# A decode step with attention and an MLP: the second MLP matrix at the end of the load stream, nine shared slots, two accumulation groups

## Chip, cores, metric

One core of one Trainium2 chip. The metric is the device time of one execution in microseconds (us), median of several runs. "Span" is the time from the first to the last instruction of the one profiled execution; it is about 1.7 us shorter than the device time. The runs come from several sessions on different chips, each with its own runs of the kernel before (medians 373.60 to 373.92 us), so a ratio compares within a session and medians of different experiments compare across chips to some 0.3 us only. Where a kernel has several runs, the trace is of one of them.

## The reference

Two branches read the same eight rows of width 576 and are mixed by a gate. In short:

```python
q = (x @ wq)                       # 8 rows, 32 heads of 128
k, v = last 2048 positions of the caches, 16 kv heads, each used by 2 heads
a = softmax(q k^T / sqrt(128)) v, all heads side by side, @ wo      # wo: 4096 x 576
b = gelu(layernorm(x) @ w1 + b1) @ w2 + b2                          # w1: 576 x 4608, w2: 4608 x 576
out = g * a + (1 - g) * b,   g = sigmoid(sum(x * gate_w))
```

The K and V windows are 2 x 67 MB; all weights together are about 20 MB. Everything is read once.

## The kernel before

It is written as a list of operations with dependencies that a small planner orders per engine. One queue (SP) issues all large loads, in the order of a list called the stream. K and V arrive in 32 units of 2 MB each, into six slots:

```python
NSLOT = 6
NJ = 4                                    # accumulation in 4 column groups of 144
stream = [("K", i) for i in range(4)] + [("M", i) for i in range(FC)]       # M: chunks of w2
stream += [("K", 4), ("W", 0), ("K", 5), ("W", 1), ("V", 0), ("W", 2), ("K", 6), ("W", 3)]   # W: chunks of wo
# ... then V and K in turn; the last V unit comes in four pieces
slot_free = [[o_qp], [o_qp], [o_qp], None, None, None]   # o_qp: the query projection is done
```

At the start slots 0 to 2 hold `wq` and slots 3 to 5 hold `w1`; `wo` has a region of its own. So the first K unit cannot be issued before the query projection has read `wq`. For each unit of K: VectorE transposes it in two halves, TensorE multiplies it with the query. For each unit of V: 64 matmuls of 8 columns. All that goes into the output (projection, `w2`, bias) is added in one PSUM bank by

```python
for i, (lhsT, rhs) in enumerate(grp.mms):
    for j in range(NJ):
        e.matmul(ps[32 * j:32 * j + 8, BK_ACC, 0:JN], lhsT, rhs[:, JN * j:JN * j + JN], ...)   # JN = 576 / NJ
```

and leaves through one VectorE copy and four output writes, two per queue (the recorded texts call them output loads).

## Time and profile before

373.74 us (373.69 to 373.95). From the page of the profile: the busy time of the engines, the rate of the loads in 40 slices of the span (9.3 us each), and the load queues (packets, megabytes, share of sixteen DMA engines' time).

```profile
PE 254.1 (68%) x3259; PEld 138.9 (37%) x3259; DVE 210.4 (57%) x253; ACT 28.3 (8%) x84; POOL 37.5 (10%) x163
...
GB/s 341 423 395 424 425 423 413 420 419 414 437 430 423 433 433 426 430 430 431 431 426 435 422 431 430 429 431 426 431 433 428 428 433 430 426 428 436 424 413 94
...
q1 hardware_dynamic: 14992, 154.28, 97.9%
q8 instruction: 25, 0.41, 0.4%
```

The rate stands at 413 to 437 GB/s in all but the first, third and last slices, and the packets of the load queue take 97.9% of the sixteen DMA engines' time, so the loads bound the kernel. A 2 MB unit lands every 4.85 us (2.097 MB / 4.85 us = 432 GB/s); this steady rate of the trace is what is called the ceiling below. What can shrink is the start, the end, and single gaps. Note the q8 line: instructions are fetched as 25 blocks of 16 KB.

Two stretches are below the rate. These are windows of the trace: start and end, length, then busy time and instruction count of PE, PEld, DVE, ACT and POOL, then the granted TensorE clock, the mean DMA share and GB/s.

```profile
24.00:30.00 6.00, 3.75 (x65) 3.09 (x62) 0.42 (x1) 1.02 (x1) 2.06 (x11) 1.00 0.89 358
...
360.00:366.00 6.00, 3.21 (x104) 2.74 (x102) 0.00 (x0) 0.00 (x0) 0.00 (x0) 0.50 0.73 302
366.00:372.00 6.00, 1.59 (x40) 1.12 (x40) 0.54 (x2) 0.00 (x0) 0.00 (x0) 0.50 0.07 25
```

The first is a gap: the query projection ends at 24.5 us, the first K loads are issued at 24.71, and before their first 2 MB packets start, at 26.24 us, the data of the load before has run out on most engines (at 26.2 us three load packets are under way, at 25.0 sixteen). The second is the end. Here is the chain of work that ended last (start, length, what):

```profile
344.39 23.61 DMA arena<-in_A_v_cache_dram
368.00 0.05 issue
368.05 0.60 PE ps L673 x16
368.65 0.02 issue
368.68 0.24 DVE arena L695
368.92 0.04 issue
368.96 0.44 PE ps L534 x7
369.40 0.02 issue
369.42 0.31 DVE arena L729
```

The last quarter of the last V unit lands at 368.0 us; then PV, normalisation, projection, eviction and output follow one after the other, to 372.1.

**A second way to read the end.** In these traces a load of 128 rows adds sixteen increments to its semaphore. I read each as one DMA engine whose share has landed; the trace does not name the engine. Their times are in the trace; the last of them is called the landing. The table below is computed from them (first, last, and the difference "spread"; in us from the start of the span):

```
                        first    last   spread
w1, large part          24.77   26.16    1.39
first K unit            31.79   32.67    0.89
last piece of V        362.73  368.00    5.27
```

Between 33 and 368 us the slowest engine has fallen more than 4 us further behind the fastest. The spread does not grow steadily. After a first rise at 38 to 43 us, behind the second and third fetch, it jumps at 146, 166, 176, 264, 284, 294 and 368 us, each time a few us after an instruction fetch (at 143, 161, 173, 261, 280, 292 and 366 us). The fetches in between leave it as it was. The jumps thus follow the first three fetches of every eight. That looked like fetches that take turns over a set of eight engines: a reading of these times, as the trace does not name the engine of a fetch.

### The profile page before, as it was taken

How to read it: one execution, taken by the hardware profiler on the slowest of the kernel's cores; microseconds unless marked ns; L12 is line 12 of the kernel's file. 1: busy time of each engine (PE TensorE's matmuls, PEld its weight loads, DVE VectorE, ACT ScalarE, POOL GpSimd, SP SyncE). 2: the span in 40 equal slices, each digit the busy share in tenths (PEclk: the TensorE clock that was granted, in tenths of full speed). 3: DMA queues.
4: the chain of work that ended last, by engine and by line, in shares of the span. 5: the costliest groups of instructions: out<-in, count | busy, mean ns of one | idle time of the engine just before them, and what ended most of it. 6: DMA issues, size and time to landing. Idle time of an engine off the chain costs nothing.

```text
span 372.1 us, 7310 instructions
## 1 busy us (share of the span) xinstructions
PE 254.1 (68%) x3259; PEld 138.9 (37%) x3259; DVE 210.4 (57%) x253; ACT 28.3 (8%) x84; POOL 37.5 (10%) x163
## 2 busy tenths in 40 slices
PE   0169995661684987496749786877859774987554
PEld 0159432230341553243324443433415332543453
DVE  1414596934159645974468646954585448754600
ACT  1010001100002000200020001100020002000300
POOL 7003011010100110010100110011001010000000
PEclk9999999695865988788886868697659666788855
DMA  8999999999999999999999999999999999999992
GB/s 341 423 395 424 425 423 413 420 419 414 437 430 423 433 433 426 430 430 431 431 426 435 422 431 430 429 431 426 431 433 428 428 433 430 426 428 436 424 413 94
DMA packets 15097, 154.77 MB, mean 416 GB/s; under 512 B 1349, under 2 KB 5462, under 8 KB 6234
## 3 DMA queue, kind: packets, MB, share of 16 engines
q1 hardware_dynamic: 14992, 154.28, 97.9%
q8 instruction: 25, 0.41, 0.4%
q10 hardware_dynamic: 74, 0.03, 0.0%
q14 instruction: 6, 0.05, 0.0%
HBM read 154.30 MB, written 0.01 MB: 415 GB/s over the span
## 4 chain that ended last, share of the span: by engine, by line
DMA 50%; DVE 25%; PE 15%; SPq 8%; issue 1%; DVEq 0%
DMA arena<-in_A_k_cache_dram 37%; DVE arena L629 15%; PE ps L643 11%; DMA arena<-in_B_w_dram 7%; DMA arena<-in_A_v_cache_dram 6%; DVE arena L595 4%; DVE arena L576 4%; SPq L666 3%; SPq L719 2%; PE ps L491 2%; SPq L614 2%; DVE arena L585 1%; DVE arena L579 1%; PE ps L493 1%; PE ps L639 0%
## 5 line engine op out<-in xcount | busy, mean ns | idle before, releaser
L629 DVE STREAM_TRANSPOSE arena<-arena 128x2048 f32<-128x2048 f32 x64 | 145.6, 2298 | 85.8 <-DMA arena<-in_A_k_cache_dram 79.9
L643 PE MATMUL ps<-arena 128*128 128x512 bf16 x512 | 161.8, 476 | 39.0 <-DVE arena L629 39.0
L643 PEld LDWEIGHTS ps<-arena 128*128 128x128 bf16 x512 | 55.5, 115 | 133.5 <-issue 55.0
L673 PEld LDWEIGHTS ps<-arena 128*128 128x128 bf16 x2048 | 56.3, 97 | 13.7 <-DMA arena<-in_A_v_cache_dram 8.5
L673 PE MATMUL ps<-arena 128*128 128x8 bf16 x2048 | 56.7, 166 | 6.8 <-DMA arena<-in_A_v_cache_dram 6.8
L622 POOL COPY arena<-arena 32x32 bf16<-32x32 bf16 x128 | 26.0, 203 | 191.4 <-PE ps L643 175.5
L639 PE MATMUL ps<-arena 128*128 128x512 bf16 x32 | 14.9, 621 | 39.6 <-DVE arena L595 33.1
L576 DVE TENSOR_REDUCE arena<-ps 128x1 f32<-128x2048 f32 x8 | 18.3, 2292 | 27.1 <-PE ps L643 27.1
L590 ACT ACTIVATE arena<-ps,arena 128x512 bf16<-128x512 f32 x32 | 21.5, 685 | 111.2 <-DVE arena L585 111.2
L595 DVE STREAM_TRANSPOSE arena<-arena 128x512 bf16<-128x512 bf16 x32 | 19.9, 676 | 0.9 <-ACT arena L590 0.9
L639 PEld LDWEIGHTS ps<-arena 128*128 128x128 bf16 x32 | 3.5, 127 | 44.7 <-DVE arena L595 33.5
L689 ACT ACTIVATE arena<-ps 128x16 f32<-128x16 f32 x15 | 2.8, 184 | 182.2 <-PE ps L673 182.2
L695 POOL TENSOR_TENSOR arena<-arena 128x16 bf16<-128x16 f32 x15 | 4.0, 264 | 121.3 <-ACT arena L689 106.6
L534 PE MATMUL ps<-arena 128*8 128x144 bf16 (+1 forms) x280 | 8.4, 235 | 6.2 <-POOL arena L695 4.9
L491 PE MATMUL ps<-arena 128*128 128x8 bf16 x144 | 10.9, 201 | 1.7 <-DMA arena<-in_B_w_dram 1.7
L491 PEld LDWEIGHTS ps<-arena 128*128 128x128 bf16 x144 | 10.8, 157 | 2.2 <-DMA arena<-in_B_w_dram 2.2
L413 PE MATMUL ps<-arena 8*128 8x8 bf16 x8 | 0.5, 167 | 12.6 <-DVE arena L386 8.8
L534 PEld LDWEIGHTS ps<-arena 128*8 128x8 bf16 (+1 forms) x280 | 3.9, 84 | 11.3 <-POOL arena L695 5.7
L695 DVE TENSOR_TENSOR arena<-ps,arena 128x16 bf16<-128x16 f32 x1 | 0.2, 228 | 13.6 <-PE ps L673 13.6
L601 DVE RECIPROCAL arena<-ps 128x32 f32<-128x32 f32 x8 | 2.8, 353 | 7.9 <-PE ps L600 7.9
L493 PE MATMUL ps<-arena 128*128 128x8 bf16 x36 | 7.2, 201 | 0.0
L600 PEld LDWEIGHTS ps<-arena 128*128 128x128 f32 x16 | 4.2, 268 | 6.6 <-DVE arena L599 4.5
(78 smaller groups left out, 76.0 us busy)
## 6 DMA issues: line engine op xcount, KB each, us to landing
arena<-in_A_k_cache_dram SPq DMA_DIRECT2D x32, 2048.0 KB, 22.8
arena<-in_A_v_cache_dram SPq DMA_DIRECT2D x31, 2048.0 KB, 24.0
arena<-in_B_w_dram SPq DMA_DIRECT2D x4, 1296.0 KB, 16.1
arena<-in_B_w_dram SPq DMA_DIRECT2D x1, 4608.0 KB, 24.4
arena<-in_A_wo_dram SPq DMA_DIRECT2D x4, 1152.0 KB, 17.6
arena<-in_A_wq_dram SPq DMA_DIRECT2D x1, 4096.0 KB, 12.8
arena<-in_A_v_cache_dram SPq DMA_DIRECT2D x4, 512.0 KB, 21.9
arena<-in_B_w_dram SPq DMA_DIRECT2D x1, 576.0 KB, 25.6
```

Of the source, the lines that this page charges most:

```text
L491: ins = e.matmul(out_, lhsT, yT[:, kt, :], start=(kt == 0), stop=False)
L493: ins = e.matmul(out_, lhsT, yT[:, 4 + c // 2, :], start=False, stop=True)
L534: ins = e.matmul(ps[32 * j:32 * j + 8, BK_ACC, 0:JN], lhsT, rhs[:, JN * j:JN * j + JN], start=False, stop=True, skip_group_check=True, til ...
L576: mx = add("dve", lambda e: e.tensor_reduce(out=k(MX), in_=ps[:, 0:4, :].rearrange("p a n -> p (a n)"), axis=AXL.X, op=ALU.max), deps=[qk_ ...
L590: return e.activation(out=Pm[:, 512 * c:512 * c + 512], in_=ps[:, c, :], func=ACTF.Exp, bias=k(NB), scale=SCALE, accum_out=k(SUM + c))
L595: pts.append(add("dve", (lambda c=c: lambda e: e.transpose(PT[:, g % 2, 16 * c:16 * c + 16, :].rearrange("p r m -> p (r m)"), Pm[:, 512 * ...
L622: return e.tensor_copy(dst, src)
L629: tr = add("dve", (lambda h=h, kb=kb: lambda e: e.transpose(bass.AP(arena_f, offset=foffs("KT") + kb * 2048, ap=[[AST // 2, 128], [1, 2048]]),
L639: mm = e.matmul(ps[:, rc, :], maskL, maskR, start=True, stop=False)
L643: mm = e.matmul(ps[:, rc, :], qbd[:, ub, 2 * h + ee, :], rhs, start=False, stop=(q == 3 and h == 1 and ee == 1))
L666: d = dma("sp", (lambda pp=pp, w=w: lambda e: e.dma_start(slot(s)[:, pp * w:(pp + 1) * w], src[:, :, pp * w:(pp + 1) * w]))(), ("t%d" % pp ...
L673: mm = e.matmul(ps[:, BK_OS[item % 2], 8 * (q % 2):8 * (q % 2) + 8], slot(s)[:, r * 128:(r + 1) * 128], PT[:, g % 2, r, 8 * q:8 * q + 8], ...
```

## The change

`w2` (5.3 MB) moves from near the start to the very end of the stream, with the bias before it. `wo` loses its own region: its four chunks pass through the slots, each behind the V units that it belongs to. The freed memory makes nine slots, and three of them are free from the start. The output is accumulated in two column groups of 288 instead of four of 144, and evicted by two engines at once. The bias matmul, which stood ahead of the query projection, now waits for a bias load behind the last projection chunk. The small piece of `wq` is loaded before the large one. The intent: fewer instructions, a shorter tail, and a stream that never waits.

```diff
-    NSLOT = 6
+    NSLOT = 9
-    NJ = 4
+    NJ = 2
-        stream = [("K", i) for i in range(4)] + [("M", i) for i in range(FC)]
-        stream += [("K", 4), ("W", 0), ("K", 5), ("W", 1), ("V", 0), ("W", 2), ("K", 6), ("W", 3)]
+        stream = [("K", i) for i in range(5)]
...                     (K and V in turn, a chunk of wo after every eighth V unit)
+        stream += [("B", 0)] + [("M", i) for i in range(FC)]
-        slot_free = [[o_qp], [o_qp], [o_qp], None, None, None]
+        slot_free = [[o_qp]] * 3 + [[o_hp]] * 3 + [[]] * 3
-            return (0, 1, 2, 0)[n] if n < 4 else (n - 3) % NSLOT
+            return (n + 6) % NSLOT
-        d_wqm = ...                                  # 4 MB, first
-        d_wqr = ... after=[d_wqm]
+        d_wqr = ...                                  # 0.5 MB, first
+        d_wqm = ... after=[d_wqr]
+            cuts = [0, 4, 7, 9] if ci == FC - 1 else [0, FJ]      # the last w2 chunk in three pieces
-        o_fin = add("dve", ... tensor_copy(out_sb[0:104, :], ps[0:104, BK_ACC, 0:JN]) ...)    # then 4 output writes
+        for j, (eng, ev) in enumerate((("sp", "dve"), ("act", "act"))):                       # one each
...                     (cut: an output tile per head pair, bias rows on 8 partitions, gate load in two)
```

More of the change, by code (lines that the diff above doesn't have):

```diff
@@ L183, in build_kernel @@
     NG = Hkv // HG
-    NSLOT = 6
+    NSLOT = 9
     SE = 4 * W
-    LEAD = 7
     FC, FJ = 4, 9
@@ L189, in build_kernel @@
     FCW = 128 * FJ
-    W2P = 5376
     WOP = 768
-    NJ = 4
+    NJ = 2
+    WO_CH = 8
     JN = D // NJ
@@ L245, in build_kernel @@
         req("o32", 2 * 16, F32)
-        req("oT", 2 * 16, BF)
+        req("oT", Hkv * 16, BF)
         req("out_sb", JN, BF)
@@ L250, in build_kernel @@
         req("KT", 2 * SE // 2, BF)
-        req("wo", Hq * WOP, BF, 512)
         req("RAW", NSLOT * SE, BF, 512)
@@ L294, in build_kernel @@
         b1T = view("b1T")
-        b2_sb = view("b2", 1)
+        b2_sb = view("b2", 8)
         u_sb, uh_sb, v1_sb, v2_sb = view("u"), view("uh"), view("v1"), view("v2")
         hT = view("hT").rearrange("p (t b) -> p t b", b=8)
-        ob = view("ob", 1)
-        ot32 = view("ot32", 1)
+        ob = view("ob", 8)
+        ot32 = view("ot32", 8)
         gb = view("gb")
@@ L305, in build_kernel @@
         o32 = view("o32").rearrange("p (u m) -> p u m", u=2)
-        oT = view("oT").rearrange("p (u h b) -> p u h b", u=2, h=2)
+        oT = view("oT").rearrange("p (u h b) -> p u h b", u=Hkv, h=2)
         out_sb = view("out_sb")
@@ L309, in build_kernel @@
         Pm = view("P")
-        wo_sb = view("wo").rearrange("p (t c) -> p t c", t=Hq)
         RAW = view("RAW")
@@ L325, in build_kernel @@
         w1_r = RAW[:, W1O + 4 * F:W1O + 4 * F + F // 2]
-        w2_sb = RAW[:, 3 * SE:3 * SE + FC * W2P].rearrange("p (c k) -> p c k", c=FC)
         def col(i, parts=128):
@@ L340, in build_kernel @@
         eng_sems = {e: es.enter_context(nc.semaphore("sem_" + e)) for e in ENGS}
-        dma_keys = ["x", "b", "wq", "w1", "wo", "out", "outb"] + ["w2_%d" % i for i in range(FC)] + ["s%d" % i for i in range(NSLOT)] + ["t%d" % i for i in range(4)]
+        dma_keys = ["x", "b", "b2", "wq", "w1", "out", "outb"] + ["s%d" % i for i in range(NSLOT)] + ["t%d" % i for i in range(4)]
         dma_sems = {k: es.enter_context(nc.semaphore("dma_" + k)) for k in dma_keys}
@@ L370, in build_kernel @@
         d_x = dma("act", lambda e: e.dma_start(x_sb, x2), "x", 8 * D * 2, name="d_x")
-        d_gw = dma("act", lambda e: e.dma_start(gw_sb, gate_w.partition_broadcast(8)), "x", 8 * D * 2, name="d_gw", after=[d_x])
+        d_gw, d_gw1 = [dma("act", (lambda r0=r0, r1=r1: lambda e: e.dma_start(gw_sb[r0:r1, :], gate_w.partition_broadcast(r1 - r0)))(), "x", (r1 - r0) * D * 2, name="d_gw%d" % r0, after=[d_x])
+                       for r0, r1 in ((0, 6), (6, 8))]
         d_b1 = dma("act", lambda e: e.dma_start(b1c, B_b1.rearrange("(c f) -> c f", c=FC)), "b", F * 2, name="d_b1", after=[d_gw])
-        d_b2 = dma("act", lambda e: e.dma_start(b2_sb, B_b2.rearrange("(o d) -> o d", o=1)), "b", D * 2, name="d_b2", after=[d_b1])
-        dx = [d_x, d_gw]
-        db = [d_b1, d_b2]
-        d_wqm = dma("sp", lambda e: e.dma_start(wq_m.rearrange("p t c -> p (t c)"), A_wq[0:512, :].rearrange("(p t) c -> p (t c)", t=4)), "wq", 512 * 8192, name="d_wqm")
-        d_wqr = dma("sp", lambda e: e.dma_start(wq_r, A_wq[512:576, :].rearrange("k (s c) -> (k s) c", s=2)), "wq", 64 * 8192, name="d_wqr", after=[d_wqm])
+        dx = [d_x, d_gw, d_gw1]
+        db = [d_b1]
+        d_wqr = dma("sp", lambda e: e.dma_start(wq_r, A_wq[512:576, :].rearrange("k (s c) -> (k s) c", s=2)), "wq", 64 * 8192, name="d_wqr")
+        d_wqm = dma("sp", lambda e: e.dma_start(wq_m.rearrange("p t c -> p (t c)"), A_wq[0:512, :].rearrange("(p t) c -> p (t c)", t=4)), "wq", 512 * 8192, name="d_wqm", after=[d_wqr])
         dwq = [d_wqm, d_wqr]
-        d_w1m = dma("sp", lambda e: e.dma_start(w1_m.rearrange("p t c -> p (t c)"), B_w1[0:512, :].rearrange("(p t) c -> p (t c)", t=4)), "w1", 512 * F * 2, name="d_w1m", after=[d_wqr])
+        d_w1m = dma("sp", lambda e: e.dma_start(w1_m.rearrange("p t c -> p (t c)"), B_w1[0:512, :].rearrange("(p t) c -> p (t c)", t=4)), "w1", 512 * F * 2, name="d_w1m", after=[d_wqm])
         d_w1r = dma("sp", lambda e: e.dma_start(w1_r, B_w1[512:576, :].rearrange("k (s c) -> (k s) c", s=2)), "w1", 64 * F * 2, name="d_w1r", after=[d_w1m])
@@ L441, in build_kernel @@
         o_gb = add("dve", lambda e: e.tensor_copy(gb, ps[:, BK_X, 384:400]), deps=[o_gp], name="gb_ev", cost=0.15)
-        o_obh = add("dve", lambda e: e.tensor_copy(ob[:, 0:8], gb[0:1, 8:16]), deps=[o_gb], name="ob_hi", cost=0.12)
+        o_obh = add("dve", lambda e: e.tensor_copy(ob[:, 0:8], dg[:, 8:16]), deps=[o_dgb], name="ob_hi", cost=0.12)
         o_ob32 = add("dve", lambda e: e.tensor_copy(ot32, ob[:, 0:8]), deps=[o_obh], name="ob_32", cost=0.12)
-        o_obl = add("dve", lambda e: e.tensor_tensor(out=ob[:, 8:16], in0=gb[0:1, 8:16], in1=ot32, op=ALU.subtract), deps=[o_ob32], name="ob_lo", cost=0.12)
+        o_obl = add("dve", lambda e: e.tensor_tensor(out=ob[:, 8:16], in0=dg[:, 8:16], in1=ot32, op=ALU.subtract), deps=[o_ob32], name="ob_lo", cost=0.12)
         o_i32 = []
@@ L541, in build_kernel @@
         NUQ = 4 * NG
-        stream = [("K", i) for i in range(4)] + [("M", i) for i in range(FC)]
-        stream += [("K", 4), ("W", 0), ("K", 5), ("W", 1), ("V", 0), ("W", 2), ("K", 6), ("W", 3)]
-        ki, vi = 7, 1
+        stream = [("K", i) for i in range(5)]
+        ki, vi = 5, 0
         while ki < NUQ or vi < NUQ:
-            if vi < NUQ:
-                stream.append(("V", vi)); vi += 1
             if ki < NUQ:
-                stream.append(("K", ki)); ki += 1
-        WO_CH = 8
-        d_woc = []
+                stream.append(("K", ki))
+                ki += 1
+            if ki >= 6:
+                stream.append(("V", vi))
+                if (vi + 1) % (NUQ // (Hq // WO_CH)) == 0:
+                    stream.append(("W", vi // (NUQ // (Hq // WO_CH))))
+                vi += 1
+        stream += [("B", 0)] + [("M", i) for i in range(FC)]
         last_dma = [d_w1r]
-        slot_free = [[o_qp], [o_qp], [o_qp], None, None, None]
+        slot_free = [[o_qp]] * 3 + [[o_hp]] * 3 + [[]] * 3
         n_slot = [0]
@@ L658, in v_unit, with pv_fn @@
             item = 2 * g + q // 2
-            final = (i == NUQ - 1)
-            src = src_of(A_v_cache, g, q)
-            parts = 4 if final else 1
-            prev = None
-            for pp in range(parts):
-                nr = 64 // parts
-                w = nr * 128
-                d = dma("sp", (lambda pp=pp, w=w: lambda e: e.dma_start(slot(s)[:, pp * w:(pp + 1) * w], src[:, :, pp * w:(pp + 1) * w]))(),
-                        ("t%d" % pp) if final else ("s%d" % s), 4 * W * Dh * 2 // parts, deps=slot_free[s] if pp == 0 else [], name="dv%d_%d" % (i, pp), after=last_dma[-1:])
-                last_dma.append(d)
-                def pv_fn(e, pp=pp, nr=nr):
-                    mm = None
-                    for r in range(pp * nr, (pp + 1) * nr):
-                        mm = e.matmul(ps[:, BK_OS[item % 2], 8 * (q % 2):8 * (q % 2) + 8], slot(s)[:, r * 128:(r + 1) * 128], PT[:, g % 2, r, 8 * q:8 * q + 8],
-                                      start=(q % 2 == 0 and r == 0), stop=(r == 63), skip_group_check=True)
-                    return mm
-                deps = [d] + pt_done[g]
-                if q % 2 == 0:
-                    deps += [o_item_ev[item - 2]] if item >= 2 else [o_qT, o_u]
-                prev = add("pe", pv_fn, deps=deps, name="pv%d_%d" % (i, pp), cost=2.2 / parts, after=[prev] + pv_hist[-1:])
+            d = dma("sp", lambda e: e.dma_start(slot(s), src_of(A_v_cache, g, q)), "s%d" % s, 4 * W * Dh * 2, deps=slot_free[s], name="dv%d" % i, after=last_dma[-1:])
+            last_dma.append(d)
+            def pv_fn(e):
+                mm = None
+                for r in range(64):
+                    mm = e.matmul(ps[:, BK_OS[item % 2], 8 * (q % 2):8 * (q % 2) + 8], slot(s)[:, r * 128:(r + 1) * 128], PT[:, g % 2, r, 8 * q:8 * q + 8],
+                                  start=(q % 2 == 0 and r == 0), stop=(r == 63), skip_group_check=True)
+                return mm
+            deps = [d] + pt_done[g]
+            if q % 2 == 0:
+                deps += [o_item_ev[item - 2]] if item >= 2 else [o_qT, o_u]
+            prev = add("pe", pv_fn, deps=deps, name="pv%d" % i, cost=2.2, after=pv_hist[-1:])
             pv_hist.append(prev)
@@ L686, in v_unit @@
                 hl = q // 2
-                pj = [proj_ops[item - 2]] if item >= 2 else []
                 if item < Hkv - 1:
@@ L690, in v_unit @@
                     o_item_ev[item] = ev
-                    eng, src_, deps = "pool", o32[:, item % 2, :], [ev, rg_done[g]] + pj
+                    eng, src_, deps = "pool", o32[:, item % 2, :], [ev, rg_done[g]]
                 else:
-                    eng, src_, deps = "dve", ps[:, bk, 0:16], [prev, rg_done[g]] + pj
+                    eng, src_, deps = "dve", ps[:, bk, 0:16], [prev, rg_done[g]]
                 def om_fn(e):
-                    return e.tensor_tensor(out=oT[:, item % 2, :, :].rearrange("p h b -> p b h"), in0=src_.rearrange("p (b h) -> p b h", h=2),
+                    return e.tensor_tensor(out=oT[:, item, :, :].rearrange("p h b -> p b h"), in0=src_.rearrange("p (b h) -> p b h", h=2),
@@ L696, in om_fn @@
                                            in1=rg[:, g % 2, 16 * hl:16 * hl + 16].rearrange("p (b h) -> p b h", h=2), op=ALU.mult)
                 oT_done[item] = add(eng, om_fn, deps=deps, name="oT%d" % item, cost=0.25, prio=9)
-                mms = [(oT[:, item % 2, h, :], wo_sb[:, 2 * item + h, 0:D]) for h in range(2)]
-                proj_ops[item] = AccGroup("proj%d" % item, mms, [oT_done[item]] + d_woc, cost=0.6, after=[g_.op for g_ in acc_groups[-1:]], prio=2).op
-        o_m2 = [AccGroup("m2_b", [(ob[:, 0:8], b2_sb), (ob[:, 8:16], b2_sb)], db + [o_obl, o_obh], cost=0.6).op]
@@ L703, in m2_chunk, with wo_chunk @@
-        def m2_chunk(ci):
-            d = dma("sp", lambda e: e.dma_start(w2_sb[:, ci, 0:FJ * D], B_w2[FCW * ci:FCW * ci + FCW, :].rearrange("(p j) n -> p (j n)", j=FJ)),
-                    "w2_%d" % ci, FCW * D * 2, deps=[o_hp], name="d_w2_%d" % ci, after=last_dma[-1:])
-            last_dma.append(d)
-            mms = [(hT[:, FJ * ci + j, :], w2_sb[:, ci, j * D:(j + 1) * D]) for j in range(FJ)]
-            o = AccGroup("m2_%d" % ci, mms, [o_hT, d], cost=2.5, after=o_m2[-1:]).op
-            o_m2.append(o)
-            for s in range(3, 6):
-                slot_free[s] = [o]
+        def wo_chunk(i):
+            s = take_slot()
+            h0 = WO_CH * i
+            dst = slot(s)[:, 0:WO_CH * WOP].rearrange("p (t c) -> p t c", t=WO_CH)
+            d = dma("sp", lambda e: e.dma_start(dst[:, :, 0:D], A_wo[128 * h0:128 * (h0 + WO_CH), :].rearrange("(t p) c -> p t c", p=128)),
+                    "s%d" % s, WO_CH * 128 * D * 2, deps=slot_free[s], name="d_wo%d" % i, after=last_dma[-1:])
+            last_dma.append(d)
+            ops = []
+            for item in range(h0 // 2, (h0 + WO_CH) // 2):
+                mms = [(oT[:, item, h, :], dst[:, 2 * item + h - h0, 0:D]) for h in range(2)]
+                ops.append(AccGroup("proj%d" % item, mms, [oT_done[item], d], cost=0.5).op)
+            slot_free[s] = ops
@@ new lines, in build_kernel, with bias @@
+        o_m2 = []
+        def bias(i):
+            d = dma("sp", lambda e: e.dma_start(b2_sb, B_b2.partition_broadcast(8)), "b2", 65536, name="d_b2", after=last_dma[-1:])
+            last_dma.append(d)
+            o_m2.append(AccGroup("m2_b", [(ob[:, 0:8], b2_sb), (ob[:, 8:16], b2_sb)], [d, o_obl, o_obh], cost=0.6).op)
+        def m2_chunk(ci):
+            s = take_slot()
+            dst = slot(s)[:, 0:FJ * D]
+            src = B_w2[FCW * ci:FCW * ci + FCW, :].rearrange("(p j) n -> p (j n)", j=FJ)
+            cuts = [0, 4, 7, 9] if ci == FC - 1 else [0, FJ]
+            ops = []
+            for n, (j0, j1) in enumerate(zip(cuts, cuts[1:])):
+                d = dma("sp", (lambda j0=j0, j1=j1: lambda e: e.dma_start(dst[:, j0 * D:j1 * D], src[:, j0 * D:j1 * D]))(),
+                        ("t%d" % n) if ci == FC - 1 else ("s%d" % s), 128 * (j1 - j0) * D * 2, deps=slot_free[s] if n == 0 else [], name="d_w2_%d_%d" % (ci, n), after=last_dma[-1:])
+                last_dma.append(d)
+                mms = [(hT[:, FJ * ci + j, :], dst[:, j * D:(j + 1) * D]) for j in range(j0, j1)]
+                ops.append(AccGroup("m2_%d_%d" % (ci, n), mms, [o_hT, d], cost=0.25 * (j1 - j0), after=o_m2[-1:]).op)
+                o_m2.append(ops[-1])
+            slot_free[s] = ops
@@ L713, in build_kernel @@
         pv_hist = []
         for kind, i in stream:
-            if kind == "M":
-                m2_chunk(i)
-            elif kind == "W":
-                h0 = WO_CH * i
-                d = dma("sp", (lambda h0=h0: lambda e: e.dma_start(wo_sb[:, h0:h0 + WO_CH, 0:D], A_wo[128 * h0:128 * (h0 + WO_CH), :].rearrange("(t p) c -> p t c", p=128)))(),
-                        "wo", WO_CH * 128 * D * 2, name="d_wo%d" % i, after=last_dma[-1:])
-                last_dma.append(d)
-                d_woc.append(d)
-            elif kind == "K":
-                k_unit(i)
-            else:
-                v_unit(i)
+            {"K": k_unit, "V": v_unit, "W": wo_chunk, "M": m2_chunk, "B": bias}[kind](i)
@@ L728, in build_kernel, with ev_fn @@
         acc_ops = [g_.op for g_ in acc_groups]
-        o_fin = add("dve", lambda e: e.tensor_copy(out_sb[0:104, :], ps[0:104, BK_ACC, 0:JN]), deps=acc_ops, name="fin", cost=0.3, prio=9)
         fin = []
-        for j in range(NJ):
-            eng = "sp" if j % 2 == 0 else "act"
-            fin.append(dma(eng, (lambda j=j: lambda e: e.dma_start(out2[:, JN * j:JN * j + JN], out_sb[32 * j:32 * j + 8, :]))(), "out" if j % 2 == 0 else "outb", 8 * JN * 2, deps=[o_fin], name="d_out%d" % j, after=last_dma[-1:]))
+        for j, (eng, ev) in enumerate((("sp", "dve"), ("act", "act"))):
+            def ev_fn(e, j=j, ev=ev):
+                dst, src = out_sb[32 * j:32 * j + 8, :], ps[32 * j:32 * j + 8, BK_ACC, 0:JN]
+                if ev == "dve":
+                    return e.tensor_copy(dst, src)
+                return e.activation(out=dst, in_=src, func=ACTF.Copy)
+            o_fin = add(ev, ev_fn, deps=acc_ops, name="fin%d" % j, cost=0.4, prio=9)
+            fin.append(dma(eng, (lambda j=j: lambda e: e.dma_start(out2[:, JN * j:JN * j + JN], out_sb[32 * j:32 * j + 8, :]))(), "out" if j == 0 else "outb", 8 * JN * 2, deps=[o_fin], name="d_out%d" % j, after=last_dma[-1:]))
```

## The prediction

> **What bounds the kernel now.** The load stream. The page's slices move 413 to 437 GB/s from the fourth to the last but one; DVE (57% busy) and PE (68%) have slack. [...] (a 2 MB K or V unit lands every 4.85 us, 432 GB/s). 154.77 MB at that rate are 358 us of the 372.1 us span. The change moves the same bytes, so only the other 14 us can shrink.
>
> **Where the 14 us are** (landing increments and packet records of the trace):
> - Head: first weight packet at 2.36 us; the first 32 KB round takes 2.0 us against 1.21 later.
> - A gap at 25 to 27 us (358 GB/s in the 24 to 30 us window): the first K loads issue at 24.7 us, after the query projection, because every slot lies under a weight matrix. Most engines lose about 0.7 us.
> - Skew between the 16 DMA engines: a unit's increments spread over 0.9 us at the start, 5.3 us at the end, in steps after 16 KB instruction fetches (25, which seem to rotate over eight engines). The last V quarter lands at 368.0 us while half the engines are idle from 363 us.
> - Tail from there: 0.60 PV, 0.23 DVE, 0.41 projection, 0.31 eviction, two output issues per queue (0.75 us), end at 372.1: 4.1 us.
>
> **What the change does.**
> 1. Slots 6 to 8 are free from the start, so three K loads queue behind the first MLP matrix: the 25 us gap goes. Worth 0 to 0.7 us; the slowest engine hardly saw it.
> 2. Small wq piece first (4 KB rows): the first round may be quicker, 0 to 0.3 us.
> 3. Accumulation in two column groups of 288 instead of four of 144: 140 matmuls and as many weight loads fewer, one 16 KB fetch fewer. The fetch at 366.6 us should go, with the last step of the skew: 0 to 0.8 us.
> 4. Tail: after the last landing, four matmuls of 288 columns (estimate 0.55 us, from 0.41 us for eight of 144), two parallel evictions (0.4), one output issue per queue (saves 0.35). The last PV, normalisation and projection move off the tail, behind 5.3 MB of second-matrix loads. 4.1 becomes about 3.0 us: saves 1.1 us.
> 5. Nine slots instead of six: nothing in the steady state, which is at its ceiling. Projection chunks (393 GB/s by landing) cost 3.0 us each wherever they stand. The bias load and matmul are hidden.
>
> All of 1 to 4 lie on the critical path but overlap in part: about 2.3 us.
>
> **Prediction: 371.4 us, 8 in 10 between 370.0 and 372.9. Faster by over 2%: 0.03; within 2%: 0.95; slower by over 2%: 0.02.**
>
> **What would show each step right or wrong.** (1) The 24 to 30 us window should show about 430 GB/s. (3) 24 instruction fetches, final spread about 4.5 us. (4) From the last second-matrix landing to the end about 3.0 us. (5) K and V units still land 4.85 us apart; PE and DVE busy nearly unchanged, DMA mean 417 to 419 GB/s.
>
> **What would make it wrong.** A slot held by a projection chunk until late projections run could stall the queue (a dip below 400 GB/s near 100, 180, 260 or 340 us). The PE order could put a projection before its chunk has landed, and stop QK behind it. The second matrix's matmuls at the halved clock could lag the stream at the end. Fetches could fall on the slowest engine once more, giving back 0.7 us or more. A gain over 2% would need the per-unit 4.85 us to fall, which I see no reason for.

The sum: 0 to 0.7, 0 to 0.3, 0 to 0.8 and 1.1 us, put at about 2.3 us together. The ranges are my estimates. The 0.4 us for the two evictions stands there without a source; they then took 0.40 and 0.45 us in the changed kernel.

## The result

371.22 us (371.06 to 371.26) against 373.72: faster by 0.7%, ratio 0.9931 with a 95% interval of 0.9914 to 0.9948. That is clear of the noise, and within 2%. A ratio here is the mean time of one kernel's runs over that of the other's in the same rounds, so it is not quite the ratio of the medians quoted. In a later session the same kernel took 371.46 us against 373.69.

The page of the changed kernel, the lines that answer to those before:

```profile
PE 242.0 (65%) x3089; PEld 137.5 (37%) x3117; DVE 210.0 (57%) x253; ACT 28.6 (8%) x85; POOL 37.5 (10%) x163
...
GB/s 343 426 422 424 427 432 431 434 424 431 429 431 429 413 436 427 429 427 429 435 426 429 414 431 432 431 431 426 426 435 433 418 424 427 435 429 426 413 420 167
...
q1 hardware_dynamic: 14848, 154.29, 98.5%
q8 instruction: 24, 0.39, 0.4%
```

One instruction fetch fewer, the third slice at 422 instead of 395, the rest as it was. (A few TensorE records are missing here.) The windows:

```profile
24.00:30.00 6.00, 2.40 (x41) 2.43 (x41) 0.00 (x0) 0.08 (x1) 3.25 (x16) 1.00 0.97 404
...
360.00:366.00 6.00, 5.17 (x44) 2.59 (x46) 0.00 (x0) 0.00 (x0) 0.00 (x0) 0.50 0.65 268
366.00:372.00 6.00, 1.11 (x14) 0.52 (x10) 0.45 (x1) 0.40 (x1) 0.00 (x0) 0.82 0.01 2
```

And the end of the chain of work that ended last:

```profile
348.28 14.82 DMA arena<-in_B_w_dram
363.11 0.04 issue
363.15 3.98 PE ps L530 x36
367.13 0.03 issue
367.15 0.05 DVEq L153
367.20 0.04 issue
367.25 0.45 DVE arena L734
```

The tail reads differently now. Before, it hung on the last landing. Now the last landing is at 366.30 us, but the chain leaves the loads at 363.1 and stays on TensorE: 36 matmuls back to back, the third and fourth chunk of `w2`, most of them at half clock (0.50 in the window). TensorE has become the last to finish.

From the landing increments, the 2.61 us of span (372.12 to 369.51) add up as follows (the tail is the time from the last landing to the end):

```
                                   before    after   gain
w1 lands, fastest engine            24.77    24.48   0.29   head
first K unit, fastest engine        31.79    30.77   1.02   head 0.29 + gap 0.73
last load, fastest engine          362.73   361.69   1.04   nothing more in 331 us
last load, slowest engine          368.00   366.30   1.70   + spread 5.27 -> 4.60, 0.67
from there to the end                4.12     3.21   0.91   tail
```

So: 0.3 us head, 0.7 us gap, 0.7 us spread, 0.9 us tail. This is bookkeeping of two traces, and the split between the fastest engine and the spread is loose: the repetition below has 362.12 and 4.27 in place of 361.69 and 4.60. The slowest engine repeats better and gives the same sum another way. Against the repetition it is 0.1 us late at the first K unit of the kernel before, 0.8 us at the third (43.29 against 42.47) and 1.6 us at the end, after the last jump of 0.8 us. The experiments ask whether the causes are the ones named.

### The profile page after: what moved, and what is told of

Read it like the earlier page. It is cut to its first block, busy times and chain, and to the rows that moved or that the text cites. A ratio compares the mean times of both kernels' runs of the same rounds, so it can differ in the third digit from the quotient of the medians.

```text
span 369.5 us, 7044 instructions
## 1 busy us (share of the span) xinstructions
PE 242.0 (65%) x3089; PEld 137.5 (37%) x3117; DVE 210.0 (57%) x253; ACT 28.6 (8%) x85; POOL 37.5 (10%) x163
## 3 DMA queue, kind: packets, MB, share of 16 engines
q1 hardware_dynamic: 14848, 154.29, 98.5%
## 4 chain that ended last, share of the span: by engine, by line
DMA 63%; PE 20%; DVE 13%; SPq 2%; issue 1%; DVEq 0%
DMA arena<-in_A_k_cache_dram 42%; PE ps L641 12%; DMA arena<-in_B_w_dram 11%; DMA arena<-in_A_v_cache_dram 10%; DVE arena L627 9%; PE ps L663 3%; DVE arena L574 2%; PE ps L487 2%; SPq L716 1%; PE ps L530 1%; PE ps L637 1%; SPq L657 1%; PE ps L489 1%; DVE arena L577 0%; DVE arena L593 0%
## 5 line engine op out<-in xcount | busy, mean ns | idle before, releaser
L641 PE MATMUL ps<-arena 128*128 128x512 bf16 x491 | 144.6, 449 | 45.1 <-DVE arena L627 44.0
L641 PEld LDWEIGHTS ps<-arena 128*128 128x128 bf16 x512 | 52.5, 109 | 129.2 <-DVE arena L627 53.2
L663 PEld LDWEIGHTS ps<-arena 128*128 128x128 bf16 x2048 | 56.1, 97 | 19.1 <-DMA arena<-in_A_v_cache_dram 14.2
L637 PE MATMUL ps<-arena 128*128 128x512 bf16 x25 | 12.3, 630 | 40.2 <-DVE arena L593 36.7
L637 PEld LDWEIGHTS ps<-arena 128*128 128x128 bf16 x32 | 3.5, 128 | 42.9 <-DVE arena L593 38.5
L530 PE MATMUL ps<-arena 128*8 128x288 bf16 (+1 forms) x140 | 14.7, 377 | 3.1 <-DMA arena<-in_B_w_dram 1.9
L487 PEld LDWEIGHTS ps<-arena 128*128 128x128 bf16 x144 | 10.8, 160 | 5.0 <-DMA arena<-in_B_w_dram 5.0
L530 PEld LDWEIGHTS ps<-arena 128*8 128x8 bf16 (+1 forms) x140 | 7.1, 106 | 10.9 <-DMA arena<-in_B_w_dram 3.6
(79 smaller groups left out, 79.4 us busy)
```

The costliest lines, as they stand in the source:

```text
L487: ins = e.matmul(out_, lhsT, yT[:, kt, :], start=(kt == 0), stop=False)
L530: ins = e.matmul(ps[32 * j:32 * j + 8, BK_ACC, 0:JN], lhsT, rhs[:, JN * j:JN * j + JN], start=False, stop=True, skip_group_check=True, til ...
L637: mm = e.matmul(ps[:, rc, :], maskL, maskR, start=True, stop=False)
L641: mm = e.matmul(ps[:, rc, :], qbd[:, ub, 2 * h + ee, :], rhs, start=False, stop=(q == 3 and h == 1 and ee == 1))
L663: mm = e.matmul(ps[:, BK_OS[item % 2], 8 * (q % 2):8 * (q % 2) + 8], slot(s)[:, r * 128:(r + 1) * 128], PT[:, g % 2, r, 8 * q:8 * q + 8], ...
```

## The experiments

All are edits of the changed kernel and give correct results. Since single effects are a few tenths of a per cent, I compare landings in the profiled run first and times second. In each table the yardstick is the unaltered changed kernel.

### The yardstick

> The changed kernel unaltered, as the yardstick for the other runs on this chip. Expected 371.2 us against 373.7 of before, a ratio of 0.993; 24 instruction fetches, the last load landing spread over 4.6 us between the DMA engines.

371.46 us (371.09 to 371.86, five runs), ratio 0.9946. First K unit at 30.81 us on the fastest engine, last load at 366.38 us, spread 4.27, tail 2.99 us. Repetition thus moves the last landing by 0.1 us on the slowest engine and 0.4 on the fastest, the spread by 0.3 and the time by up to 0.4 from the median. The trace of the yardstick is of its fastest run, 371.09 us.

### What closed the gap at 25 us?

In the changed kernel the query projection ends at 21.3 us, 3.2 us earlier than before: the small loads of the second queue land earlier (the load of `b1`, for which TensorE waited until 13.5 us, now lets it go at 11.6, 1.9 us), and the bias matmul no longer stands ahead of it in TensorE's order (the other 1.3 us). Loads issued on its end would then come in time even without free slots. Two edits tell these apart.

```diff
 e1:  slot_free = [[o_qp]] * 3 + [[o_hp]] * 3 + [[o_qp]] * 3      # was [[]] * 3 at the end
 e8:  as e1, and four idle VectorE operations (0.75 us each) that the query projection waits for
```

> The changed kernel, but slots 6 to 8 count as free only when the query projection is done, as all slots did before. Theory A, of the prediction (the free slots close the gap at 25 us): the gap comes back, the first K unit lands 0.7 us later on the fastest engine, and the kernel takes 371.7 to 371.9 us. Theory B (the gap closed because the query projection now ends at 21.3 us instead of 24.5, so that K loads issued on its end come in time anyway): no gap, 371.2 us within 0.1.

> As e1, and four idle vector operations of about 0.75 us delay the query projection by 3 us, to where it ended before. Both theories expect the gap back here: the first K unit 0.7 us later, 371.8 to 372.0 us, if most engines pass their loss on to the end. If only the slowest engine matters and it had no gap, 371.2 to 371.4 us. With e1 at 371.2 and e8 at 371.9, theory B stands and the free slots are only a second cure of the same gap.

```
                  median   ratio     first K, fastest   last load, slowest   tail
yardstick         371.46   0.9946         30.81               366.38         2.99
e1                372.17   0.9957         30.98               366.67         3.78
e8                373.67   1.0001         32.59               368.46         3.39
before            373.69                  31.79               368.00         4.12
```

e8, the window of the gap:

```profile
24.00:30.00 6.00, 5.48 (x114) 5.00 (x112) 0.42 (x1) 1.02 (x1) 1.42 (x7) 1.00 0.81 314
```

Without free slots the gap stays closed but for 0.2 us (theory B; the first K load is issued at 22.63 us there); it opens when the projection is late as well. The padding run below (e6, 128 matmuls) has the projection late (its end lets go the next K loads at 28.10 us) and the free slots kept, and its first K unit lands at 30.83: no gap. So either cure is enough, and the change contains both. e1's median is 0.7 us up, and the intervals of the two ratios overlap (0.9946 to 0.9969, and 0.9933 to 0.9959). Its profiled run is 1.1 us above the yardstick's: 0.3 in the landing and 0.8 in the tail, which is treated below.

e8 also settles a point of the prediction. Its gap is wider than that of before (first loads issued at 25.57 us instead of 24.71), and the slowest engine loses 1.75 us at the first K unit and still 2.1 us at the last load. In this run, then, the gap in the stream was not made good later. That the slowest engine "hardly saw it" does not hold in the trace of the kernel before either, past the first unit: against the yardstick it is late, head included, by 0.11 us at the first K unit, but by 0.61 at the second and 0.82 at the third.

### The instruction fetches

```diff
 e3:  NJ = 4, with the eviction and the four output writes of before (about 280 TensorE instructions more)
 e6:  a block of 128 (or 32) useless matmuls into an unused bank, ahead of the query projection
```

> The changed kernel, but accumulating in four column groups of 144 with one eviction and four output loads as before, which brings back some 280 instructions of TensorE. Theory of the prediction: 25 fetches instead of 24, the last spread 0.7 us wider (5.3 instead of 4.6), and the tail after the last landing 0.2 to 0.4 us longer (second output issue): 372.1 to 372.3 us. Rival (the number of fetches does not matter, only the tail does): 371.4 to 371.6 us with the spread at 4.6.

> The changed kernel with 128 useless matmuls (256 TensorE instructions, about 4 us) ahead of the query projection, in time where TensorE waits and the stream has K loads queued in the free slots. Fetch theory: one instruction fetch more (25), falling near 355 to 360 us on the same engine as the first, ninth and seventeenth; the last spread grows by about 1.0 to 1.3 us, and the kernel takes 372.3 to 372.8 us where the unaltered one took 371.4. Rival (what the fewer matmuls gave was TensorE time or a shorter tail): no difference, 371.3 to 371.6 us. If the free slots do close the gap, the first K unit lands at 30.8 us although the query projection is late.

> Control for the padding: 32 useless matmuls (64 instructions) in the same place, too few for one fetch more before the stream ends. Fetch theory: 24 fetches, spread 4.3 to 4.6 us, 371.3 to 371.6 us. If each added instruction costs in itself, a quarter of what the 128 cost.

The queue line of the page, of the three in this order:

```profile
q8 instruction: 26, 0.43, 0.4%
```

```profile
q8 instruction: 25, 0.41, 0.4%
```

```profile
q8 instruction: 25, 0.41, 0.4%
```

```
              median  ratio   fetches ended before  spread   last load,   last load,   tail
                              the last load landed           fastest      slowest
yardstick     371.46  0.9946         24              4.27      362.12       366.38     2.99
e3            372.87  0.9979         25              5.78      361.97       367.75     3.20
pad of 128    373.14  0.9984         25              5.25      362.47       367.72     3.65
pad of 32     371.84  0.9945         24              4.33      362.02       366.35     3.78
```

This is the clearest result. One fetch more while the stream is still running, whether by real work (e3, at 360 us) or by padding alone, puts the slowest engine's last landing back by 1.37 and 1.34 us, while the fastest engine's moves by -0.15 and +0.35. In the control the twenty-fifth fetch starts at 365.84 us, half a microsecond before the last landing: no effect on landings. The first two edits share only that they add some 260 to 280 TensorE instructions, in different places and for different work. That it is the fetch, and not the instructions as such, is seen in time. In e3 the spread goes from 4.36 to 5.80 us with the fetch at 360 us. In the padding run the slowest engine is 0.1 us ahead of the yardstick's at the landing at 346 us, 0.5 behind after the fetch at 345 and 1.3 behind after the one at 355. So the fetches are shown to be a cause of the spread. The spread jumps by 1.2 to 1.5 us at the ninth and seventeenth fetch (1.18 and 1.19 in the first trace of the changed kernel, 1.33 and 1.36 in the yardstick, 1.45 and 1.49 in e3); I read that as the least that a fetch of 16 KB costs the DMA engine that carries it. A 16 KB packet of data takes 0.61 us and the packet of the fetch itself 0.88 to 0.97 (the traces of the kernel before and of the changed one). As an estimate from these jumps, eight engines with three such fetches each, of 24, come to some 4 us, which is the lag at the end: in the yardstick's last load eight increments come at 362.12 to 363.98 us and eight at 366.11 to 366.38. From the loads of this kernel, whose packets take 98.5% of the DMA engines' time, the fetch is not hidden.

The fetches are not all of one price for the end: as I read it, what counts is whether the engine that pays is last, or becomes last by it. In the kernel before the spread jumped with three of every eight, in e3 by over 0.3 us with one of every eight only.

### Head, stream order, number of slots

```diff
 e2:  the 4 MB piece of wq first, as before
 e5:  w2 and the bias behind the fifth K unit; the last wo chunk before the last V unit; last V unit in four pieces
 e4:  NSLOT = 6
```

> The changed kernel, but the 4 MB piece of the query weights goes first, as before. Theory of the prediction: the first round of 32 KB packets takes 2 us again, the first MLP matrix lands 0.2 to 0.3 us later, and so does everything after: 371.6 to 371.8 us where the unaltered one took 371.4. Rival: nothing, the head is hidden.

> The changed kernel with nine slots, two column groups and interleaved projection chunks, but the second MLP matrix is loaded early (behind the fifth K unit) and V ends the stream, its last unit in four pieces as before. Theory: the last load lands at the same time within 0.3 us, and the tail holds PV, normalisation and projection again, 0.5 to 0.9 us more than 3.1: 372.0 to 372.4 us. Rival (the order of the stream changes the stream itself): the last landing moves by over 0.5 us.

> The changed kernel with six slots instead of nine, all of them under a weight matrix at the start. Theory of the prediction (depth gives nothing in the steady state): units still land 4.85 us apart, no stall; as e1 then, 371.4 to 372.2 us. Rival (the nine slots keep the queue full where six would not, since projection chunks now hold slots as well): gaps of over 0.3 us between landings, over 372.5 us.

```
              median  ratio   last load, fastest   last load, slowest   tail
yardstick     371.46  0.9946       362.12               366.38          2.99
e2            371.62  0.9946       362.25               366.74          3.04
e5            372.19  0.9958       361.94               366.40          4.06
e4            372.59  0.9973       363.87               368.52          3.10
```

**e2.** The weights land 0.24 us later, as expected; at the end that is 0.1 to 0.4 us, and in the times it drowns in the scatter (ratios equal). The head is real in the landings and not proven in the times.

**e5.** The order of the stream as such does not move the last landing (366.40 against 366.38). It moves the tail, by 1.1 us. Its last instructions:

```profile
366.45 0.59 PE L673 MATMUL ps<-arena 128*128 128x8 bf16 x16 [0.61 <-DMA arena<-in_A_v_cache_dram]
367.07 0.23 DVE L695 TENSOR_TENSOR arena<-ps,arena 128x16 bf16<-128x16 f32 x1 [15.80 <-PE ps L673]
...
367.36 0.65 PE L530 MATMUL ps<-arena 128*8 128x288 bf16 x4 [0.32 <-DVE arena L695]
368.04 0.45 DVE L752 CAST arena<-ps 8x288 bf16<-8x288 f32 x1 [0.74 <-PE ps L530]
```

PV, normalisation and projection again stand between landing and eviction. Moving the second matrix behind them is worth about a microsecond against the yardstick's tail of 2.99 us, but only 0.3 us against the tails of 3.78 us that other runs show (see the clock below). The prediction's 1.1 us was for this and the two evictions and output writes together; e5 has those already, so the agreement is in size only.

**e4.** Six slots cost 1.1 us in the median (across chips) and 2.1 us at the last landing of the profiled run, which was the slowest of its five (373.35 us); the prediction did not foresee it. It is not the steady state: units land 4.85 us apart in both. On the slowest engine the yardstick and e4 part at one place, the unit whose first share lands at 84 us in the yardstick: its last lands at 86.16 us there and at 88.27 in e4, and from there on e4 is 2.1 us late, to the end. The window there, of e4 and then of the yardstick:

```profile
78.00:84.00 6.00, 5.91 (x85) 3.46 (x85) 5.23 (x3) 0.18 (x1) 1.07 (x5) 1.00 0.98 369
```

```profile
78.00:84.00 6.00, 6.00 (x118) 3.92 (x115) 5.23 (x3) 0.19 (x1) 1.42 (x7) 1.00 1.00 426
```

And the issues of e4's queue ahead of it:

```profile
57.40 0.54 SPq L612 DMA_DIRECT2D arena<-in_A_k_cache_dram  x1
65.92 0.54 SPq L657 DMA_DIRECT2D arena<-in_A_v_cache_dram  x1
76.93 0.54 SPq L612 DMA_DIRECT2D arena<-in_A_k_cache_dram  x1
```

Two issues 11 us apart, where a unit takes 4.85 us to load: the slot waits for VectorE, which is held up by the first softmax, and with six slots the queue then holds no more than the rest of one unit, which lands at 79.77 to 81.49 us. Five of the first 16 KB packets of the late unit, at 79.4 to 79.6 us, take 1.4 to 2.7 us each. No other 16 KB packet between 30 and 340 us takes over 1.2 us in this trace. Why the late unit starts so slowly is not shown. The nine-slot kernel has such waits too (issues at 65.1 and 75.6 us), with three more units queued in front of them. The kernel before may not have needed this, since its 10 MB of `w2` and `wo` in the early stream gave the compute time to catch up; the nine slots would then be the price of moving those loads away. No run with six slots and the early loads kept tests that.

### The tail and the clock of TensorE

Over the runs that end with `w2`, leaving out the fillers below and e3 (other instructions), the tail after the last landing is either 3.0 to 3.2 us or 3.65 to 3.8 us (and 3.4 once), with almost the same instructions. The last matmuls in the timeline of the yardstick, and of e1:

```profile
363.23 3.72 PE L530 MATMUL ps<-arena 128*8 128x288 bf16 x36 [0.75 <-DMA arena<-in_B_w_dram]
```

```profile
363.56 4.49 PE L530 MATMUL ps<-arena 128*8 128x288 bf16 x36 [0.77 <-DMA arena<-in_B_w_dram]
```

And a window inside them, again of the yardstick and of e1 (the clock is the last figure but two):

```profile
366.00:367.00 1.00, 0.95 (x16) 0.44 (x10) 0.00 (x0) 0.00 (x0) 0.00 (x0) 0.99 0.00 0
```

```profile
366.00:367.00 1.00, 1.00 (x12) 0.57 (x10) 0.00 (x0) 0.00 (x0) 0.00 (x0) 0.50 0.05 18
```

The same 36 matmuls take 3.72 us where the clock is granted in full from 366 us, and 4.49 us where it stays at half. The clock records of the traces hold two values, 0.50 and 1.00, and all changes of the clock within one trace lie whole multiples of 3.41 us apart, on a grid that falls differently in each (the first change on record is at 44.06 us in the kernel before and at 42.16 in the changed kernel). In the yardstick a step of this grid falls at 366.02 us, 2.8 us into the matmuls, and the clock rises. In e1 the steps fall at 365.59 us, 2.0 us into them, without a rise, and at 369.00 us, after their end. What makes the clock rise is not shown. It goes with work, without a sharp limit: in the traces of the kernel before and of the changed one all 38 rises follow a step of the grid in which TensorE (matmuls or weight loads) was busy for a share of 0.71 or more, and of the 39 steps after which the clock stayed at 0.50, 38 have a share of 0.69 or less and one has 0.80. In these runs, the later the rise comes after the last landing, the longer the tail was: 2.99 us for a rise 0.36 us before it, 3.21 for 0.12 after, 3.39 for 0.43, 3.65 for 0.98, 3.78 for 1.36 (yardstick, changed kernel, e8, pads of 128 and 32).

### Two attempts at a faster version

If the end is set by engines that lag, and always the same ones, bytes can be moved to the others; so I reasoned. First, which are they? In the trace a load of few rows, n, adds one increment at the issue and n as the data lands (the bias load of the changed kernel, of 8 rows: one at 317.64 us and eight from 349.38 to 353.65). I took it that n engines carry it, and that a load of one row more uses the same engines and one more. This is an assumption: the trace does not name the engines.

```diff
 e7:   loads of 2, 3, ... 15 rows of 128 bytes, each with its own semaphore, before the bias load
 e9:   w1[.., 8192:18432] in rows 0-111, then 112-116, 117-121, 122-126 (five rows each), then row 127
 e10:  as e9, and 4 filler matmuls of 512 columns ahead of the first three chunks of w2 (1, 1, 2)
```

> The changed kernel with fourteen tiny loads of 2 to 15 rows just before the bias load near the end, each with a semaphore of its own, so that their increments show how far behind each DMA engine is[...]. Fetch theory: about eight engines lag by 3 to 4.6 us and the others by under 1.5 us, and the laggards are a fixed set; if they are mostly the higher-numbered ones, shifting bytes to the lower ones would bring the end forward. Rival: the lag is spread evenly over all, with no set to be named. No change of time expected beyond 0.5 us.

> The changed kernel, but 16 of the 128 rows of a 20 KB wide part of the first MLP matrix are loaded five at a time[...]. Theory (the time is set by the DMA engines that lag, and the lag is a fixed set): the last load lands 0.5 to 0.8 us earlier, at 365.6 to 365.9 us, the final spread falls to 3.5 to 3.9, and the kernel takes 370.6 to 370.9 us where the unaltered one took 371.4. Rival (the engines share one limit, so moving bytes moves nothing): 371.3 to 371.6 us.

> As e9, and four filler matmuls of 512 columns fill TensorE's waits between the chunks of the second MLP matrix, so that its clock is granted in full before the last chunk. In the runs so far the tail after the last landing was 3.0 to 3.2 us where the clock came up before the end and 3.7 to 3.8 us where it did not. Theory: tail 2.6 to 2.9 us in every run, the runs scatter less, 370.0 to 370.5 us. Rival (the tail is set by the evictions and output writes alone): as e9.

Five increments of a small load came early, and if loads of five rows always go to those five engines, the other eleven have 20 KB each less to carry. That is some 0.77 us, an estimate from the 0.61 us of a 16 KB packet. In e10, that filling TensorE's waits brings its clock up is likewise a theory.

**e7 (one look).** By what each load adds to the one before, about 350 us, with the engines numbered from 0 in the order in which the loads add them: engines 0 to 4, 7 and 8 were at 349.4 to 351.6 us, 10 at 352.3, and 5, 6, 9 and 11 to 14 at 353.6 to 353.8. Seven are clearly late and an eighth is half-way, which fits fetches that take turns over eight engines, with the third turn of the eighth, the 24th fetch at 352.3 us, still to come. 15 was not probed, but is early by elimination: the chunk of `wo` just ahead has eight increments at 349.2 to 351.4 us, one at 352.2 and seven at 353.4 to 353.6. The numbering stands on the assumption of nested loads. The probe also carries a warning: in it each tiny load delayed its engines by about 0.18 us, though it moved 128 bytes per row. Fourteen of them brought the final spread down to 1.98 us, and yet the last landing was 0.9 us later (367.30): the nested loads held back the early engines most, which narrowed the spread, but the late engines 5 and 6 too, nine or ten times each.

**e9** failed: 379.81 us, ratio 1.0159. The windows of the head:

```profile
18.00:24.00 6.00, 5.06 (x156) 4.37 (x152) 0.43 (x1) 0.38 (x1) 0.00 (x0) 1.00 1.02 290
24.00:30.00 6.00, 0.00 (x0) 0.00 (x0) 0.00 (x0) 0.64 (x1) 3.27 (x16) 1.00 1.13 195
30.00:36.00 6.00, 0.00 (x0) 0.00 (x0) 0.00 (x0) 0.00 (x0) 0.00 (x0) 1.00 0.91 137
```

The engines are busy all through (share 1.02, 1.13, 0.91) at 137 to 290 GB/s. Already while the load of 112 rows is under way the rate falls (205 to 328 GB/s between 19 and 26 us), and further under the five-row loads after it (108 to 153 GB/s between 28 and 36 us); the first K unit is 9 us late. In the first two of those windows the changed kernel, with the 128-row form, ran at 396 and 404 GB/s. Why the rate falls is not shown, nor which of the two shapes costs how much. The final spread was 4.10. Whether moving bytes can help is therefore untested: the edit broke something larger than it mended.

**e10** carries the same fault (377.89 us), so its time says nothing. Its fillers did in the profiled run what they were for:

```profile
367.00:368.00 1.00, 0.85 (x13) 0.54 (x14) 0.00 (x0) 0.00 (x0) 0.00 (x0) 0.73 0.92 389
368.00:369.00 1.00, 1.00 (x12) 0.34 (x8) 0.00 (x0) 0.00 (x0) 0.00 (x0) 1.00 1.01 421
```

The clock came up in it almost six microseconds before the last landing (367.55 and 373.42 us), TensorE then waited for the pieces again, and the tail was 2.87 us against 3.75 in e9. One trace each; the fillers alone, in the kernel that wins, were not run and stay an open proposal. An estimate of their worth from these two tails is up to 0.9 us, on those executions whose clock stays down. No version tried beats the changed kernel.

## Why the prediction was right

Forecast 371.4 us (370.0 to 372.9) and "within 2%" at 0.95; measured 371.22. The sum was 2.3 us; the medians differ by 2.5, the spans by 2.6. That it came so close is in part luck: gap, head and fetches came out at or near the top of their ranges, the tail less than forecast, and a clock that stays down would have added some 0.6 us (3.78 against 3.21). Two times in it stand 0.5 to 0.6 us later than in the trace (the first weight packet starts at 1.82 us, the last fetch at 366.01); nothing rests on them. The terms:

1. **Gap, "0 to 0.7 us".** It gained 0.7, at the top of the range. The reason for the low end of the range was wrong ("the slowest engine hardly saw it"): by the third K unit the slowest engine had lost 0.8 us, head included, and e8 shows that such a loss lasts. And the free slots are only one of two cures; the earlier query projection is the other (e1), which the prediction did not see, and in the change itself the two cannot be told apart. Its check, 430 GB/s in the 24 to 30 us window, failed (404), although the landings show no gap: 4.85 us from the last part of `w1` (25.92) to the first K unit (30.77) on the fastest engine. Landings were the better test.
2. **Head, "0 to 0.3".** 0.29 in the traces, 0.24 at the same landing in e2; not resolved in the times. The first sixteen 32 KB packets take 1.21 to 1.41 us each in the changed kernel, 1.43 to 2.18 before.
3. **Fetches, "0 to 0.8".** 24 fetches and a spread of 4.60, as forecast (4.5); 0.67 us (1.0 against the repetition). Confirmed twice by adding one back, which cost more (1.3 to 1.4) than its removal had gained. That is no contradiction: in the kernel before, the last fetch fell on an engine that was not the last one, so that part of its cost did not show. In the increments of the piece before, one of the eight late engines stands ahead of the rest (365.09 us, the others 365.76 to 365.98); in the last piece that place is empty, and one engine stands behind the rest (368.00, the others 366.99 to 367.18).
4. **Tail, "1.1 us, to about 3.0".** 0.91, to 3.21 (1.13 against the repetition); e5 finds 1.1 for the order of the stream alone. The mis-sized term is "four matmuls, 0.55 us": TensorE does not wait for the last piece, it is still working through 36 matmuls at half clock, 3.98 us from the landing of the third chunk. The prediction had listed this under what would make it wrong ("could lag the stream at the end"); it happens, and costs 0.2 us or 0.8 us as the clock has it.
5. **"Nine slots: nothing in the steady state".** True as worded (4.85 us per unit), but it was counted as nothing at all. With six slots this stream loses 2.1 us near 80 us in the profiled run (e4; 1.1 us in the median). The step that failed is the assumption that a stream at its ceiling in one order stays there in another with the same slots. That the early weight loads of the old order served as padding is argued, not shown.

Most of the hazards that were named did not occur: no dip below 400 GB/s appears in the page's slices between the first and the last, the mean is 419 GB/s as forecast, and no QK stood behind a projection for long enough to show there.

## What to carry to other kernels

In this kernel, whose loads ran at their ceiling, the mean rate hid what the times of a load's sixteen increments showed: some came 4.3 to 4.6 us after the first, and the compute on a load began with its latest (third chunk of `w2`: last increment at 363.11, first matmul at 363.15 us). The fetching of instructions counted there too: one fetch more put the last landing back by 1.34 and 1.37 us, so fewer instructions shortened a kernel whose compute engines had time to spare (PE 65% and DVE 57% busy). In another kernel, look at the same times. Put last in the stream what needs the least work after landing (here a tail of 4.06 us in e5, against 2.99 to 3.78 where `w2` ends the stream), but check that its work is not slowed by an engine at half clock (3.78 us in two runs), and that the loads moved away were not what kept the queue full at the start (with six slots the changed order lost 2.1 us near 80 us; that the early loads would have prevented it is not shown).
